# Block-summary attention and two MLPs in one kernel: mask added by a product, v summed on GpSimd, loads and steps placed anew

## Chip, cores and metric

One core of one Trainium2 chip runs the program. The time is device microseconds of one execution; the median of three runs is given, and the profile is of one further execution.

## The reference, cut to what matters

Two batches of 8 heads, 768 positions, head size 64. Keys are summarised per block of 32 by their maximum, values by their mean; each query sees keys less than 16 positions away and all 24 summaries. Then a gated MLP (512 to 1536 to 512) and a squared-relu MLP (512 to 2048 to 512) on the 1536 tokens.

```python
k_sum = k.reshape(B, H, nb, block, D).max(axis=3)
v_sum = v.reshape(B, H, nb, block, D).mean(axis=3)
scores_l = scale * np.matmul(q, k.transpose(0, 1, 3, 2))
mask_l = np.abs(pos[:, None] - pos[None, :]) < window
scores_s = scale * np.einsum('bhsd,bhnd->bhsn', q, k_sum) + np.log(block)
scores_all = np.concatenate([np.where(mask_l, scores_l, -1e9), scores_s], axis=-1)
a = np.exp(scores_all - np.max(scores_all, axis=-1, keepdims=True))
a = a / (np.sum(a, axis=-1, keepdims=True) + 1e-09)
x = np.matmul(a, np.concatenate([v, v_sum], axis=2))
g = x @ w_gate
x = (g * (1.0 / (1.0 + np.exp(-g))) * (x @ w_val)) @ w_out
h = np.maximum(x @ w_in, 0.0)
return h * h @ w2_out
```

## The kernel before

**Work and order.** The tokens are three sets of 512. Attention of a set is four pairs of heads, each with two units of 256 queries. The weights arrive as 64-bit floats in chunks; VectorE and ScalarE turn the words into fp32 by integer pieces (`convert`, L152 to L181: abs, clamp, shift, sign, low), and split each value into a high and a low fp32r part (`split_chunk`, L197), so that every product is three matmuls. Converted chunks are written to DRAM (`keep_chunk`) and read again (`load_kept`) for the later sets.

**Prologue (L516 to L623).** Attention of set 0 runs as a loop over t, written out by hand: in iteration t unit t+1 has its scores, unit t its mask and exps, unit t-1 its reciprocals, normalisation and transposes, unit t-2 the copy of the transposed weights (`turned`), unit t-3 its product with v, unit t-4 the split of the result into x high and x low. Between them stand the v sums, the k maxima (`sum_k`, `fill_k`) and the conversion of chunks 0 and 1 (`tick`). `begin` multiplies the first chunk's parts as soon as their x is there.

**Steps (L642 to L707).** Step k works on weight chunk k: 12 for each set in the gated MLP ("12"), then 16 for each set in the second MLP ("34"). A step has three slots, n = 3k, 3k+1, 3k+2: the gate product with silu (L681), the value product with g = g * p (L683) and the split of g into `hh` and `hl` (L684, L685), and the second-layer block of the step before (`second`, L486 or L488). In each slot `first`, `after` and `late` hold the attention steps of the next set, placed by `place` (L427 to L448): for pair hp of the next set s = d0 + 6 hp + 4, scores at s and s+1, product at s+9 and s+10. `pieces_of` runs the conversion of chunk k+2 and the split of chunk k+1 in the slots. All loads go out on SP's queue, in the order of the program; each engine runs its own instructions in that order too.

**v sums.** `sum_v` (L256) sums v over 32 positions with 24 matmuls of a 0/1 matrix `sel` (scaled by 1/32); `keep_v` copies the result to `vs`, and `load_vs` (L313) spreads it from there into the last 24 rows of the v tile by a DMA that repeats each row.

**Masks.** `masked` (L349) is one VectorE pass a block, which adds the mask to the scores from PSUM, writes them negated to SBUF and keeps their minimum; `exps` (L363) reads that copy.

The lines in the profile: L262 v sums, L344 scores, L357 mask pass, L368 exps, L381 and L387 normalisation, L393 transposes, L397 their copy, L405 product with v, L412 and L416 x high and low, L460 first-layer products, L209 the low part of a weight chunk, L177 and L172 the sign and low pieces, L328 and L336 k maxima, L376 reciprocal.

Of the kernel before, what the change touches and what calls it, by code (L numbers as in the profile page):

```python
# [24 lines left out]
def block_summary_attention__gated_mlp__relu2_mlp(  # L25
# [13 lines left out]
    P = 128  # L39
# [43 lines left out]

    VG = 3
    VT = 4 * S // P
    sel = const.tile([P, VG, 4 * NS], F32, name="sel")

# [168 lines left out]
    def sum_v(b, g, pool):  # L256

        n = 4 * NS
        t = vn_t.pop((b, g))
        ps = bank(pool)  # L260
        for i in range(VT):
            nc.tensor.matmul(  # L262
                ps[0:n, 0:D], sel[:, i * VG // VT, :], t[:, i * D:(i + 1) * D],
                start=(i == 0), stop=(i == VT - 1),
            )
        vs_t[b, g] = ps

    def keep_v(b, g):
        n = 4 * NS
        ps = vs_t[b, g]  # L270
        vs = vs_t[b, g] = sm_p.tile([P, D], F32, tag="vs", name="vs")
        nc.vector.tensor_copy(vs[0:n, :], ps[0:n, 0:D])

    class Pair:
# [28 lines left out]
        def load_q(self):  # L303
            self.q = att_p.tile([P, 2 * UB, P], F32, tag="q", name="q", bufs=3)
            for b, bk, at, n in self.runs():
                nc.sync.dma_start(out=self.q[:, at:at + n, :], in_=qB[b, self.hp, :, bk:bk + n, :])
# [6 lines left out]
        def load_vs(self):  # L313
            for b, bk, at, n in self.runs():
                for j in range(2):
                    h = 2 * self.hp + j
                    r = (h % 4) * NS
                    nc.sync.dma_start(
                        out=self.v[WIN:W, at:at + n, j * D:(j + 1) * D],
                        in_=vs_t[b, h // 4][r:r + NS, :].unsqueeze(1).to_broadcast([NS, n, D]),  # L320
                    )
# [26 lines left out]

        def masked(self, j):  # L349
            ps = self.st.pop(("ps", j))  # L350
            s = self.st["s", j] = att_p.tile([P, 512], F32, tag="s", name="s", bufs=3)
            m = self.st["m", j] = sm_p.tile([P, UB], F32, tag="m", name="m")
            for i in range(UB):
                bk = self.units[j][1] * UB + i
                mv = 0 if bk == 0 else (2 if bk == NBK - 1 else 1)
                c = slice(i * W, (i + 1) * W)
                nc.vector.tensor_tensor_reduce(  # L357
                    out=s[:, c], in0=ps[:, c], in1=mask[:, mv, :],
                    scale=-SCALE, scalar=3.0e38, op0=ALU.add, op1=ALU.min,
                    accum_out=m[:, i:i + 1],  # L360
                )

        def exps(self, j):  # L363
            s, m = self.st["s", j], self.st.pop(("m", j))
            r = self.st["r", j] = sm_p.tile([P, UB], F32, tag="r", name="r")
            for i in range(UB):
                c = slice(i * W, (i + 1) * W)
                nc.scalar.activation(  # L368
                    s[:, c], s[:, c], ACTF.Exp, bias=m[:, i:i + 1], scale=-1.0,
                    accum_out=r[:, i:i + 1],  # L370
                )

        def recip(self, j):
            r = self.st["r", j]
            nc.vector.tensor_scalar_add(r, r, 1e-9)
            nc.vector.reciprocal(r, r)  # L376
# [33 lines left out]
        def high(self, j):  # L410
            ts = slice(j * UT, (j + 1) * UT)
            nc.scalar.copy(self.x[0][self.hp][:, ts], self.st["po", j][:, 0:UT])  # L412
# [13 lines left out]
    def place(i, x):  # L426

        d0 = (i - 1) * 3 * F1
        pairs = [Pair(i, hp, x) for hp in range(NP)]
        for hp, p in enumerate(pairs):  # L430
            s = d0 + 6 * hp + 4
            at(first, s - 9, p.load_k)
            at(first, s - 8, p.load_q)
            at(first, s - 4, p.sum_k)
            at(first, s - 3, lambda p=p: p.fill_k(nc.vector))
            at(first, s - 4, p.load_v)
            at(first, s + 5, p.load_vs)
            for j in range(2):
                at(after, s + j, lambda p=p, j=j: p.scores(j))
                at(first, s + j + 1, lambda p=p, j=j: p.masked(j))  # L440
                at(late, s + 3, lambda p=p, j=j: p.exps(j))
                at(first, s + 6, lambda p=p, j=j: p.recip(j))
                at(after, s + 6, lambda p=p, j=j: p.norm_act(j))
                at(after, s + 7 + j, lambda p=p, j=j: p.turn(j, ps_a))
                at(first, s + 8 + j, lambda p=p, j=j: p.turned(j))
                at(after, s + 9 + j, lambda p=p, j=j: p.product(j, ps_a))
                at(first, s + 10 + j, lambda p=p, j=j: p.high(j))
                at(first, s + 10 + j, lambda p=p, j=j: p.low(j))  # L448
# [56 lines left out]
    with tc.manual_schedule():  # L505
# [15 lines left out]
        pairs[1].load_q()  # L521
        make_identity(nc, ident)
# [23 lines left out]
        load_words(0)  # L546
        pairs[2].load_k()
        pairs[2].load_q()
# [16 lines left out]

        for t in range(n_u + 4):
            if t == 0:
                go("scores", 0)
            go("high", t - 4)
            if t == 0:  # L570
                load_vn(0, 1)
                pairs[1].load_v()
            elif t == 1:
                pairs[3].load_k()
                pairs[3].load_q()
            elif t == 2:
                pairs[0].load_vs()
                pairs[1].load_vs()
                pairs[2].load_v()
                load_words(1)  # L580
            elif t == 4:
                pairs[2].load_vs()
                pairs[3].load_v()
                load_words(2)
            elif t == 5:
                pairs[3].load_vs()
            go("scores", t + 1)
            if t in (0, 2):
                sum_v(0, t // 2, ps_m)
            go("masked", t)  # L590
# [30 lines left out]
            tick(2)  # L621
# [20 lines left out]
        for k in range(NK):  # L642
# [25 lines left out]
            if kind == "12":  # L668
                h = new_h()
                for j in range(2):  # L670
# [100 lines left out]
```

## Time and profile before

| | |
|---|---|
| runs | 681.62, 683.2, 685.67 us (median 683.2) |
| the profiled execution | 683.89 us, span 681.8 us (2.1 us lie around it) |
| mean granted TensorE clock | 0.967 |
| TensorE busy | 646.6 us (95%) |
| VectorE, ScalarE, GpSimd busy | 414.3 (61%), 347.3 (51%), 13.1 us (2%) |
| DMA moved | 126.03 MB |

Times are microseconds from the span's start. PE is TensorE's matmuls and PEld its weight loads, DVE is VectorE, ACT ScalarE, POOL GpSimd, SP the queue that issues DMAs. The granted clock is the share of full speed (2.4 GHz) that TensorE was given. An fp32 matmul of this kernel shows as two records. A wait for several things is put down to the one that came last by the profile; where the engine that it names had long been done, it was another, often a DMA.

### The profile page before, as it was taken

To read this page: it belongs to the slowest core of one execution; us is meant where nothing else is said; L and a number is where in the kernel's file an instruction comes from. 1 tells how busy PE (TensorE), PEld (TensorE's weight loads), DVE (VectorE), ACT (ScalarE), POOL (GpSimd) and SP (SyncE) were. 2 spreads that over 40 slices of the span, in tenths; PEclk is the share of its full clock that TensorE was granted. 3 is DMA by queue.
4 is the path that set the end of the run, shared out by engine and by line. 5 is a ranking of instruction groups with operands and counts; after the bars stand their busy time and mean duration, and the time that the engine had idled before them with its cause. 6 is when DMAs were issued, how large, how long until landed. Compare 5 with 4: busy or idle time off the path is not lost.

```text
span 681.8 us, 9023 instructions
## 1 busy us (share of the span) xinstructions
PE 646.6 (95%) x3312; PEld 534.8 (78%) x3312; DVE 414.3 (61%) x686; ACT 347.3 (51%) x622; POOL 13.1 (2%) x26
## 2 busy tenths in 40 slices
PE   5758997979999999999999999999999999999997
PEld 5746886868788778788888888888888888888885
DVE  3277977967857666576866766444454454544443
ACT  3364476666744887674544334444444444444442
POOL 2120000000000000000000000000000000000000
PEclk9677998979999999999999999999999999999999
DMA  8998659593498587537576533222324222252211
GB/s 332 310 313 295 225 201 331 190 315 137 163 357 269 188 284 262 191 139 249 214 267 239 174 124 123 93 94 103 109 96 156 92 93 93 92 175 104 93 46 63
DMA packets 52908, 126.03 MB, mean 185 GB/s; under 512 B 9856, under 2 KB 16000, under 8 KB 51328
## 3 DMA queue, kind: packets, MB, share of 16 engines
q1 hardware_dynamic: 52864, 125.46, 53.3%
q8 instruction: 26, 0.43, 0.3%
q14 instruction: 18, 0.15, 0.1%
HBM read 103.28 MB, written 20.97 MB: 182 GB/s over the span
## 4 chain that ended last, share of the span: by engine, by line
PE 84%; DMA 6%; DVE 4%; ACT 4%; issue 2%; SPq 1%; POOLq 0%; DVEq 0%; ACTq 0%
PE bank L460 25%; PE bank L469 19%; PE bank L488 19%; PE bank L486 14%; PE bank L262 2%; DMA vn<-in_vN_dram 2%; PE bank L405 2%; PE bank L344 2%; DMA v<-vs 1%; PE bank L393 1%; DMA wf<-kept 1%; DMA q<-in_qB_dram 1%; DVE wlo L209 1%; ACT wf L158 1%; ACT s L368 1%
## 5 line engine op out<-in xcount | busy, mean ns | idle before, releaser
L209 DVE TENSOR_TENSOR wlo<-wf,whi 128x1024 fp32r<-128x1024 f32 (+2 forms) x85 | 122.0, 1435 | 50.9 <-ACT whi L208 50.2
L208 ACT CAST whi<-wf 128x1024 fp32r<-128x1024 f32 (+2 forms) x85 | 104.2, 1226 | 78.7 <-PE bank L488 50.8
L460 PE MATMUL bank<-xh,whi 128*128 128x512 f32 x288 | 116.8, 406 | 2.3 <-ACT g L681 2.3
L460 PE MATMUL bank<-xl,whi 128*128 128x512 f32 x288 | 113.6, 394 | 0.0
L460 PE MATMUL bank<-xh,wlo 128*128 128x512 f32 x288 | 113.4, 394 | 0.0
L695 DVE TENSOR_TENSOR r<-r 128x512 f32<-128x512 f32 x48 | 33.2, 692 | 87.0 <-ACT hh L694 87.0
L488 PE MATMUL bank<-whi,hl 128*128 128x512 f32 x192 | 74.8, 390 | 0.0
L488 PE MATMUL bank<-whi,hh 128*128 128x512 f32 x192 | 74.7, 389 | 0.0
L488 PE MATMUL bank<-wlo,hh 128*128 128x512 f32 x192 | 74.7, 389 | 0.0
L469 PE MATMUL bank<-xh,whi 128*128 128x512 f32 x192 | 74.7, 389 | 0.0
L469 PE MATMUL bank<-xl,whi 128*128 128x512 f32 x192 | 74.7, 389 | 0.0
L469 PE MATMUL bank<-xh,wlo 128*128 128x512 f32 x192 | 74.7, 389 | 0.0
L693 ACT ACTIVATE r<-bank 128x512 f32<-128x512 f32 x48 | 28.7, 598 | 87.3 <-PE bank L469 87.3
L460 PEld LDWEIGHTS bank<-xh,whi 128*128 128x128 f32 x288 | 55.0, 191 | 14.0 <-ACT g L681 2.7
L684 ACT CAST hh<-g 128x512 fp32r<-128x512 f32 x36 | 22.3, 619 | 85.2 <-DVE g L683 85.2
L460 PEld LDWEIGHTS bank<-xh,wlo 128*128 128x128 f32 x288 | 54.8, 190 | 11.9 <-DVE wlo L209 0.2
L460 PEld LDWEIGHTS bank<-xl,whi 128*128 128x128 f32 x288 | 55.0, 191 | 10.6
L486 PE MATMUL bank<-hh,whi 128*128 128x512 f32 x144 | 59.7, 415 | 0.0
L486 PE MATMUL bank<-hl,whi 128*128 128x512 f32 x144 | 58.0, 403 | 0.0
L486 PE MATMUL bank<-hh,wlo 128*128 128x512 f32 x144 | 57.7, 401 | 0.0
L368 ACT ACTIVATE s<-s,m 128x120 f32<-128x120 f32 x96 | 36.6, 382 | 17.2 <-DVE m L357 17.1
L177 DVE SCALAR_TENSOR_TENSOR wf<-raw,wf 128x1024 uint32<-128x1024 uint32 (+2 forms) x29 | 42.3, 1457 | 0.1
(60 smaller groups left out, 898.8 us busy)
## 6 DMA issues: line engine op xcount, KB each, us to landing
wf<-kept SPq DMA_DIRECT2D x120, 256.0 KB
raw<-in_w_dram SPq DMA_DIRECT2D x44, 512.0 KB
kept<-wf SPq DMA_DIRECT2D x28, 512.0 KB
raw<-in_w_dram SPq DMA_DIRECT2D x12, 1024.0 KB
wf<-kept SPq DMA_DIRECT2D x24, 512.0 KB
kw<-in_kW_dram SPq DMA_DIRECT2D x8, 768.0 KB
q<-in_qB_dram SPq DMA_DIRECT2D x8, 512.0 KB
vn<-in_vN_dram SPq DMA_DIRECT2D x4, 768.0 KB
```

Of the source, the lines that this page charges most:

```text
L177: nc.vector.scalar_tensor_tensor(out=w, in0=lw, scalar=29, in1=w, op0=ALU.logical_shift_right, op1=ALU.bitwise_or)
L208: lambda: nc.scalar.copy(hi[:, cs], t),
L209: lambda: nc.vector.tensor_sub(lo[:, cs], t, f32(hi[:, cs])),
L262: nc.tensor.matmul(ps[0:n, 0:D], sel[:, i * VG // VT, :], t[:, i * D:(i + 1) * D], start=(i == 0), stop=(i == VT - 1),)
L368: nc.scalar.activation(s[:, c], s[:, c], ACTF.Exp, bias=m[:, i:i + 1], scale=-1.0, accum_out=r[:, i:i + 1],)
L460: nc.tensor.matmul(p, w[a][:, c], x[i][kk], start=(kk == 0 and n == 0), stop=(kk == KD - 1 and n == 2),)
L469: nc.tensor.matmul(p, w[a][:, c], x[i][kk], start=(kk == 0 and n == 0), stop=(kk == KD - 1 and n == 2),)
L486: nc.tensor.matmul(ps[t], w[a][:, c], h[e], start=(f == 0 and n == 0), stop=(f == last and n == 2))
L488: nc.tensor.matmul(ps[t], h[e][:, t * P:(t + 1) * P], w[a][:, off:off + DM], start=(f == 0 and n == 0), stop=(f == last and n == 2),)
L684: nc.scalar.copy(h[0], g)
L693: nc.scalar.activation(r, p, ACTF.Relu)
L695: nc.vector.tensor_mul(r, r, r)
```

## The change

- **Prologue scores.** `masked_scores` adds the mask on TensorE, as a second product into the same bank (identity times mask); `tops` takes the maxima by one VectorE reduction and scales them; `masked_exps` reads the scores from PSUM. The steps keep `masked` and `exps`.
- **v sums.** `sum_v` is now three halving additions on GpSimd; `mean_v` sums the last partials by three matmuls. `vs` is one constant tile.
- **Prologue order.** SP's loads are in another order (chunk 0, k and q of pair 2, v of pair 1 and the second v group ahead of the setup; chunk 1 at t=0); `load_vs` goes to ScalarE's queue at t=0 and t=5; the second v sum moves to t=4 and t=5; chunk 0's conversion starts at t=2 and its pieces are spread by one or two an iteration.
- **Steps.** k loads at s-4 (were s-9), q at s-6 (s-8), v at s-3 (s-4), vs at s+7 (s+5); `sum_k` and `fill_k` late in s-2 (s-4, s-3), `fill_k` on GpSimd; one `recips` for two units; turn, copy and product one slot later; x high on VectorE. Weight loads move from the head of the step to slot 1, the keep from there to slot 2. In the "12" steps the sign piece moves between the cast of `hh` and the subtraction for `hl`. In step 0 the abs of chunk 2 comes behind the silu, clamp and shift in slot 1. The second batch's v loads go out in slot 0 and are summed late in slots 1 and 3.

```diff
...
-    def sum_v(b, g, pool):
-        n = 4 * NS
-        t = vn_t.pop((b, g))
-        ps = bank(pool)
-        for i in range(VT):
+    def sum_v(b, g, engine):
+        t = vn_t[b, g].rearrange("p (s c d) -> p s c d", s=VG, d=D)
+        n = VT // VG // 2
+        while n:
+            engine.tensor_add(t[:, :, 0:n, :], t[:, :, 0:n, :], t[:, :, n:2 * n, :])
+            n //= 2
+    def mean_v(b, g, pool):
+        t = vn_t.pop((b, g)).rearrange("p (s c d) -> p s c d", s=VG, d=D)
+        ps = vs_t[b, g] = bank(pool)
+        for i in range(VG):
             nc.tensor.matmul(
-                ps[0:n, 0:D], sel[:, i * VG // VT, :], t[:, i * D:(i + 1) * D],
-                start=(i == 0), stop=(i == VT - 1),
-            )
-        vs_t[b, g] = ps
+                ps[0:4 * NS, 0:D], sel[:, i, :], t[:, i, 0, :], start=(i == 0), stop=(i == VG - 1)
...
-        def load_vs(self):
+        def load_vs(self, queue):
             for b, bk, at, n in self.runs():
                 for j in range(2):
                     h = 2 * self.hp + j
                     r = (h % 4) * NS
-                    nc.sync.dma_start(
+                    queue.dma_start(
...
+        def masked_scores(self, j):
+            ps = self.st["ps", j] = bank(ps_a)
+            for i in range(UB):
+                c = slice(i * W, (i + 1) * W)
+                nc.tensor.matmul(ps[:, c], self.q[:, j * UB + i, :], self.kw[j][:, i, 0:W], start=True, stop=False)
+                nc.tensor.matmul(ps[:, c], ident, mask[:, self.variant(j, i), :], start=False, stop=True)
...
+        def tops(self, j):
+            m = self.st["m", j] = sm_p.tile([P, UB], F32, tag="m", name="m")
+            ps = self.st["ps", j]
+            nc.vector.tensor_reduce(
+                out=m, in_=ps[:, 0:UB * W].rearrange("p (n c) -> p n c", c=W), op=ALU.max, axis=AX.X
+            )
+            nc.vector.tensor_scalar_mul(m, m, -SCALE)
...
+        def masked_exps(self, j):
+            ps, m = self.st.pop(("ps", j)), self.st.pop(("m", j))
+            s = self.st["s", j] = att_p.tile([P, 512], F32, tag="s", name="s", bufs=4)
+            r = self.st["r", j] = sm_p.tile([P, UB], F32, tag="r", name="r")
+            for i in range(UB):
+                c = slice(i * W, (i + 1) * W)
+                nc.scalar.activation(
+                    s[:, c], ps[:, c], ACTF.Exp, bias=m[:, i:i + 1], scale=SCALE,
+                    accum_out=r[:, i:i + 1],
+                )
...
+        def recips(self):
+            r = self.st.pop("rr")
...
-        def high(self, j):
+        def high(self, j, copy):
             ts = slice(j * UT, (j + 1) * UT)
-            nc.scalar.copy(self.x[0][self.hp][:, ts], self.st["po", j][:, 0:UT])
+            copy(self.x[0][self.hp][:, ts], self.st["po", j][:, 0:UT])
...
             s = d0 + 6 * hp + 4
-            at(first, s - 9, p.load_k)
-            at(first, s - 8, p.load_q)
-            at(first, s - 4, p.sum_k)
-            at(first, s - 3, lambda p=p: p.fill_k(nc.vector))
-            at(first, s - 4, p.load_v)
-            at(first, s + 5, p.load_vs)
+            at(first, s - 4, p.load_k)
+            at(first, s - 6, p.load_q)
+            at(late, s - 2, p.sum_k)
+            at(late, s - 2, lambda p=p: p.fill_k(nc.gpsimd))
+            at(first, s - 3, p.load_v)
+            at(first, s + 7, lambda p=p: p.load_vs(nc.sync))
             for j in range(2):
                 at(after, s + j, lambda p=p, j=j: p.scores(j))
                 at(first, s + j + 1, lambda p=p, j=j: p.masked(j))
                 at(late, s + 3, lambda p=p, j=j: p.exps(j))
-                at(first, s + 6, lambda p=p, j=j: p.recip(j))
+                if j == 0:
+                    at(first, s + 6, p.recips)
                 at(after, s + 6, lambda p=p, j=j: p.norm_act(j))
-                at(after, s + 7 + j, lambda p=p, j=j: p.turn(j, ps_a))
-                at(first, s + 8 + j, lambda p=p, j=j: p.turned(j))
-                at(after, s + 9 + j, lambda p=p, j=j: p.product(j, ps_a))
-                at(first, s + 10 + j, lambda p=p, j=j: p.high(j))
-                at(first, s + 10 + j, lambda p=p, j=j: p.low(j))
+                at(after, s + 8 + j, lambda p=p, j=j: p.turn(j, ps_a))
+                at(late if j else first, s + 9, lambda p=p, j=j: p.turned(j))
+                at(after, s + 10 + j, lambda p=p, j=j: p.product(j, ps_a))
+                at(first, s + 11 + j, lambda p=p, j=j: p.high(j, nc.vector.tensor_copy))
+                at(first, s + 11 + j, lambda p=p, j=j: p.low(j))
...
+        load_words(0)
+        pairs[2].load_k()
+        pairs[2].load_q()
+        pairs[1].load_v()
+        load_vn(0, 1)
...
-        load_words(0)
-        pairs[2].load_k()
-        pairs[2].load_q()
...
+        sum_v(0, 0, nc.gpsimd)
         for t in range(n_u + 4):
             if t == 0:
-                go("scores", 0)
-            go("high", t - 4)
+                go("masked_scores", 0)
+            go("high", t - 4, nc.scalar.copy)
             if t == 0:
-                load_vn(0, 1)
-                pairs[1].load_v()
-            elif t == 1:
                 pairs[3].load_k()
                 pairs[3].load_q()
-            elif t == 2:
-                pairs[0].load_vs()
-                pairs[1].load_vs()
                 pairs[2].load_v()
                 load_words(1)
             elif t == 4:
-                pairs[2].load_vs()
                 pairs[3].load_v()
                 load_words(2)
-            elif t == 5:
-                pairs[3].load_vs()
-            go("scores", t + 1)
-            if t in (0, 2):
-                sum_v(0, t // 2, ps_m)
-            go("masked", t)
+            go("masked_scores", t + 1)
+            go("tops", t)
+            if t in (0, 5):
+                mean_v(0, t // 5, ps_m)
+                keep_v(0, t // 5)
+            go("recip", t - 1)
+            go("norm", t - 1)
             if t % 2 == 0 and t // 2 + 1 < NP:
                 pairs[t // 2 + 1].sum_k()
                 pairs[t // 2 + 1].fill_k(nc.gpsimd)
-            if t in (1, 3):
-                keep_v(0, t // 2)
-            go("recip", t - 1)
-            go("norm", t - 1)
+            if t == 4:
+                sum_v(0, 1, nc.gpsimd)
             go("product", t - 3, ps_c)
-            go("exps", t)
+            go("masked_exps", t)
             go("low", t - 4)
             go("turned", t - 2)
-            if t == 3:
+            if t in (0, 5):
+                pairs[t // 5 * 2].load_vs(nc.scalar)
+                pairs[t // 5 * 2 + 1].load_vs(nc.scalar)
+            if t == 2:
                 pieces += convert_chunk(0)
+                tick()
+            elif t == 3:
+                tick(2)
             elif t == 5:
                 tick(len(pieces))
                 pieces += split_chunk(0)
...
                 tick(len(pieces))
                 pieces += convert_chunk(1)
                 begin(0, 0)
+            elif t == 7:
+                keep_chunk(0)
+                begin(1, 0)
+                tick()
             elif t == 8:
-                keep_chunk(0)
                 load_words(3)
-                begin(1, 0)
+                tick()
             elif t == 9:
                 begin(0, 1)
                 begin(1, 1)
             elif t == 11:
                 begin(0, 2)
                 begin(1, 2)
-            tick(2)
+            tick()
             go("turn", t - 1, ps_c)
...
-        load_vn(1, 0)
-        load_vn(1, 1)
         for g in range(2):
-            at(after, 7 + g, lambda g=g: sum_v(1, g, ps_a))
+            at(first, 0, lambda g=g: load_vn(1, g))
+            at(late, 1 + 2 * g, lambda g=g: sum_v(1, g, nc.gpsimd))
+            at(after, 7 + g, lambda g=g: mean_v(1, g, ps_a))
             at(first, 8 + g, lambda g=g: keep_v(1, g))
         cv = {2: convert_chunk(2)}
-        cv[2][0]()
...
-            load_words(k + 4)
-            keep_chunk(k + 1)
             sp, c2 = split_chunk(k + 1), cv.pop(k + 2)
-            work = [sp[0:1] + c2[1:3], sp[1:2] + c2[3:4], c2[4:5]]
+            if k:
+                work = [sp[0:1] + c2[1:3], sp[1:2], c2[4:5]]
+            else:
+                work = [sp[0:1], sp[1:2] + c2[1:3], c2[4:5]]
             def pieces_of(*slots):
                 nonlocal ticks
                 for s in slots:
                     for f in work[s]:
                         f()
+                    if s == 1:
+                        load_words(k + 4)
                     if s == 2:
+                        keep_chunk(k + 1)
                         load_kept(k + 3)
                         cv[k + 3] = convert_chunk(k + 3)
                         cv[k + 3][0]()
...
                         nc.scalar.activation(g, p, ACTF.Silu)
+                        if k == 0:
+                            c2[0]()
                     else:
                         nc.vector.tensor_mul(g, g, p)
                         nc.scalar.copy(h[0], g)
+                        c2[3]()
                         nc.vector.tensor_sub(h[1], g, f32(h[0]))
...
```

## Rows read from the trace of the kernel before

**Rows 1.** Busy times by stretch: PE, PEld, DVE, ACT, POOL (instructions), clock, DMA share, GB/s.

```profile
6.80:59.60 52.80, 41.00 (x333) 36.16 (x333) 27.44 (x101) 22.87 (x82) 9.75 (x14) 0.74 0.95 329
72.80:174.30 101.50, 94.10 (x564) 78.23 (x563) 77.87 (x148) 65.70 (x138) 0.00 (x0) 0.93 0.68 237
112.80:119.60 6.80, 6.19 (x28) 4.84 (x28) 2.24 (x3) 6.73 (x20) 0.00 (x0) 0.50 0.93 340
140.10:146.90 6.80, 6.13 (x28) 4.96 (x28) 2.65 (x3) 6.10 (x19) 0.00 (x0) 0.50 0.95 355
146.90:676.00 529.10, 526.44 (x2541) 433.16 (x2540) 314.05 (x452) 267.01 (x431) 0.00 (x0) 1.00 0.46 158
```

**Rows 2.** Timeline, TensorE: first scores and last product of the prologue.

```profile
6.79 3.73 PE L344 MATMUL bank<-kw,q 128*128 128x120 f32 x16 [6.79 <-DVE kw L336]
...
58.89 0.69 PE L405 MATMUL bank<-a,v 120*64 120x64 f32 x16
```

**Rows 3.** Chain that ended last, in order of time: start, us, what.

```profile
21.62 7.94 PE bank L262 x48
...
73.06 2.74 PE bank L486 x12
...
103.20 10.07 DMA v<-vs
...
174.33 2.72 PE bank L486 x12
```

**Rows 4.** Groups by line and shape: operands, count, busy us, mean ns, idle before.

```profile
L357 DVE CUSTOM_DVE_ANT_0 s<-bank,mask 128x120 f32<-128x120 f32 x96 | 21.2, 277 | 3.4 <-PE bank L344 3.4
...
L262 PE MATMUL bank<-vn,sel 128*96 128x64 f32 x192 | 20.6, 278 | 3.8 <-DMA vn<-in_vN_dram 3.8
...
L177 DVE SCALAR_TENSOR_TENSOR wf<-raw,wf 128x1024 uint32<-128x1024 uint32 x17 | 21.5, 1266 | 0.1
...
L416 DVE TENSOR_TENSOR xl<-bank,xh 128x256 fp32r<-128x256 f32 x24 | 10.0, 416 | 31.5 <-ACT xh L412 31.5
...
L412 ACT CAST xh<-bank 128x256 fp32r<-128x256 f32 x24 | 8.5, 363 | 8.8 <-PE bank L405 8.8
...
L328 DVE TENSOR_REDUCE ks<-kw 128x24 f32<-128x768 f32 x8 | 7.6, 949 | 5.5 <-DMA kw<-in_kW_dram 5.5
...
L376 DVE RECIPROCAL r<-r 128x4 f32<-128x4 f32 x24 | 4.3, 178 | 0.8
```

**Rows 5.** Waits of TensorE: who waited for whom, us, times, longest.

```profile
PE bank L405 <- DVE hl L685: 3.7, 1, 3.7
...
PE bank L405 <- DMA v<-vs: 3.0, 1, 3.0
...
PE bank L344 <- ACT a L397: 2.7, 3, 1.3
```

**Rows 6.** Timeline, SP's queue: issues of vs.

```profile
103.20 3.35 SPq L318 DMA_DIRECT2D v<-vs  x4
...
130.45 3.70 SPq L318 DMA_DIRECT2D v<-vs  x4
```

**Rows 7.** Waits of SP's queue.

```profile
SPq L294 <- PE bank L344: 34.1, 3, 13.7
```

**Rows 8.** Timeline, VectorE: product g of steps 1, 2 and 3.

```profile
75.82 0.68 DVE L683 TENSOR_TENSOR g<-g,bank 128x512 f32<-128x512 f32 x1
...
87.38 0.68 DVE L683 TENSOR_TENSOR g<-g,bank 128x512 f32<-128x512 f32 x1
...
100.42 0.68 DVE L683 TENSOR_TENSOR g<-g,bank 128x512 f32<-128x512 f32 x1
```

**Rows 9.** Timeline, GpSimd and VectorE side by side in the prologue.

```profile
38.88 0.99 POOL L381 TENSOR_TENSOR s<-s,r 128x480 f32<-128x480 f32 x1 [2.35 <-DVE r L376]
...
38.94 2.01 DVE L177 SCALAR_TENSOR_TENSOR wf<-raw,wf 128x1024 uint32<-128x1024 uint32 x1
```

**Rows 10.** Waits of VectorE.

```profile
DVE hl L685 <- ACT hh L684: 28.4, 36, 3.1
```

More of the change, by code (lines that the diff above doesn't have):

```diff
@@ L86, in block_summary_attention__gated_mlp__relu2_mlp @@
     sel = const.tile([P, VG, 4 * NS], F32, name="sel")
+    vs = const.tile([P, 2, 2, D], F32, name="vs")
     def new_x():
@@ L254, in load_vn @@
         nc.sync.dma_start(out=t, in_=vN[b, g].rearrange("r m -> (r m)").rearrange("(p m) -> p m", p=P))
-    def sum_v(b, g, pool):
-        n = 4 * NS
-        t = vn_t.pop((b, g))
-        ps = bank(pool)
-        for i in range(VT):
+    def sum_v(b, g, engine):
[8 more added lines that the diff above has]
+        for i in range(VG):
             nc.tensor.matmul(
-                ps[0:n, 0:D], sel[:, i * VG // VT, :], t[:, i * D:(i + 1) * D],
-                start=(i == 0), stop=(i == VT - 1),
+                ps[0:4 * NS, 0:D], sel[:, i, :], t[:, i, 0, :], start=(i == 0), stop=(i == VG - 1)
             )
-        vs_t[b, g] = ps
     def keep_v(b, g):
[L269 to L272, printed above, removed]
+        nc.vector.tensor_copy(vs[0:4 * NS, b, g, :], vs_t.pop((b, g))[0:4 * NS, 0:D])
     class Pair:
@@ L303, in load_q @@
         def load_q(self):
-            self.q = att_p.tile([P, 2 * UB, P], F32, tag="q", name="q", bufs=3)
+            self.q = att_p.tile([P, 2 * UB, P], F32, tag="q", name="q", bufs=2)
             for b, bk, at, n in self.runs():
@@ L317, in load_vs @@
                     r = (h % 4) * NS
-                    nc.sync.dma_start(
+                    queue.dma_start(
                         out=self.v[WIN:W, at:at + n, j * D:(j + 1) * D],
-                        in_=vs_t[b, h // 4][r:r + NS, :].unsqueeze(1).to_broadcast([NS, n, D]),
+                        in_=vs[r:r + NS, b, h // 4, :].unsqueeze(1).to_broadcast([NS, n, D]),
                     )
@@ L347, in scores, with variant @@
                 )
+        def masked_scores(self, j):
[4 more added lines that the diff above has]
+                nc.tensor.matmul(ps[:, c], ident, mask[:, self.variant(j, i), :], start=False, stop=True)
+        def variant(self, j, i):
+            bk = self.units[j][1] * UB + i
+            return 0 if bk == 0 else (2 if bk == NBK - 1 else 1)
+        def tops(self, j):
[15 more added lines that the diff above has]
+                )
         def masked(self, j):
             ps = self.st.pop(("ps", j))
-            s = self.st["s", j] = att_p.tile([P, 512], F32, tag="s", name="s", bufs=3)
+            s = self.st["s", j] = att_p.tile([P, 512], F32, tag="s", name="s", bufs=4)
             m = self.st["m", j] = sm_p.tile([P, UB], F32, tag="m", name="m")
             for i in range(UB):
-                bk = self.units[j][1] * UB + i
-                mv = 0 if bk == 0 else (2 if bk == NBK - 1 else 1)
+                mv = self.variant(j, i)
                 c = slice(i * W, (i + 1) * W)
@@ L364, in exps @@
             s, m = self.st["s", j], self.st.pop(("m", j))
-            r = self.st["r", j] = sm_p.tile([P, UB], F32, tag="r", name="r")
+            if j == 0:
+                self.st["rr"] = sm_p.tile([P, 2 * UB], F32, tag="rr", name="rr")
+            r = self.st["r", j] = self.st["rr"][:, j * UB:(j + 1) * UB]
             for i in range(UB):
@@ L374, in recip @@
             r = self.st["r", j]
+            nc.vector.tensor_scalar_add(r, r, 1e-9)
+            nc.vector.reciprocal(r, r)
+        def recips(self):
+            r = self.st.pop("rr")
             nc.vector.tensor_scalar_add(r, r, 1e-9)
@@ L441, in place @@
                 at(late, s + 3, lambda p=p, j=j: p.exps(j))
-                at(first, s + 6, lambda p=p, j=j: p.recip(j))
+                if j == 0:
+                    at(first, s + 6, p.recips)
                 at(after, s + 6, lambda p=p, j=j: p.norm_act(j))
-                at(after, s + 7 + j, lambda p=p, j=j: p.turn(j, ps_a))
-                at(first, s + 8 + j, lambda p=p, j=j: p.turned(j))
-                at(after, s + 9 + j, lambda p=p, j=j: p.product(j, ps_a))
-                at(first, s + 10 + j, lambda p=p, j=j: p.high(j))
-                at(first, s + 10 + j, lambda p=p, j=j: p.low(j))
+                at(after, s + 8 + j, lambda p=p, j=j: p.turn(j, ps_a))
[3 more added lines that the diff above has]
+                at(first, s + 11 + j, lambda p=p, j=j: p.low(j))
     def run(d, n):
```

## The prediction

> **What bounds the kernel now.** I read the busy times by stretch first. From 147 us on TensorE is busy 526.4 of 529.1 us at full clock [rows 1]. What can be won lies before that, in two stretches: the prologue, which ends with its last attention product at 59.6 [rows 2], and the eight steps from the second-layer block of step 1 (73.06) to that of step 9 (174.33) [rows 3]. A step is one weight chunk k; the eight take 101.5 us.
>
> In the **prologue** TensorE is busy 41.0 of 52.8 us, but at a mean granted clock of 0.74, and VectorE only 27.4 [rows 1]. In the chain of waits one piece stands out: the 48 matmul records that sum v for heads 4 to 7, 7.94 us from 21.62 on [rows 3], all other work behind them. All 192 records of v sums take 20.6 us [rows 4]; the other three groups thus take 4.2 each, one in the prologue and two (8.4) in the steps.
>
> In the **eight steps** TensorE is busy 94.1 of 101.5 us [rows 1]. Its long waits are two: 3.0 us for the broadcast of vs, and 3.7 put down to VectorE's L685; three later ones for ScalarE's copy of a are 1.3 at most [rows 5]. I read the 3.7 as the broadcast too: SP issued vs at 103.20 and at 130.45 [rows 6], each about 10 us before a stop ended, and for the first the chain names 10.07 us of that transfer [rows 3]. Around the end of each stop the granted clock falls to 0.50 (the 1.2 GHz level) for 6.8 us, in which TensorE works 6.19 and 6.13 us [rows 1]; half of that, 6.2, is lost. The short waits lie in the stretch granted 1.00 throughout [rows 1, 5]. Why is vs late? SP's queue runs in order, and a k load in it stands up to 13.7 us, 34.1 in three times, for the scores that free its buffer [rows 7]; the weight loads, keeps and vs behind it then go out together.
>
> VectorE is the next limit. From the product g of step 1 (75.82) to that of step 2 it needs 11.56 us, to that of step 3 (100.42) 24.6 for two steps [rows 8].
>
> **The change, part by part.**
>
> *v sums.* A group falls from 48 records to 6, at 20.6/192 = 0.11 us each 0.65. In the steps TensorE drops 8.4 and gets 1.3 back. Its bare need there is then 94.1 - 8.4 - 6.2 + 1.3 = 80.8 us, 10.1 a step. The sums become three GpSimd additions of 768, 384 and 192 elements per partition: by its product of 480 elements in 0.99 us [rows 9], 1344 x 0.99/480 = 2.8 us a group. VectorE pays beside it: L177 took 2.01 us over that product [rows 9] against a mean of 1.27 [rows 4], so 0.74 of 0.99. I charge 0.75 x 2.8 = 2.1 us a group, between nothing (operations that GpSimd doesn't disturb) and the whole 2.8. The Trainium skill ("SBUF — State Buffer", Who interferes with whom) speaks against the move: the ports that these two engines share are, it says, locked for a whole instruction. By it VectorE would stand 2.8 us a group, some 3 us more over the four groups; the additions themselves are in no run here.
>
> *Prologue scores.* The mask becomes a second product of the same shape: 8 more records a unit. The first 16 took 3.73 us [rows 2], so 1.9 us a unit at worst; at 0.11 a record it is 0.9. Over eight units 7 to 15 us of TensorE, I take 11, against 7.9 + 4.2 - 1.3 = 10.8 of sums that go: even. On VectorE one reduction of 480 columns (768 take 0.95, so 0.6) with a small scaling replaces four masked passes of 0.28 that overlap [rows 4]: even, at most 0.5 a unit less. For exp from PSUM the nearest row is ScalarE's cast of 256 PSUM columns in 0.36 [rows 4]; an exp of 120 costs at most that much more than from SBUF, or something less; between the two I take no difference. The scores' bank is now held until the exps end; the scores two units on wait for that.
>
> *New waits.* mean_v on TensorE waits for GpSimd's sum, at t=0 (behind it the scores of unit 2) and t=5 (the product of unit 2). The vs transfers go to ScalarE's queue and wait for keep_v; behind them stand the next unit's exps. Eight issues at 0.84 (3.35 for four [rows 6]) are 6.7 us of ScalarE, busy 22.9 of 52.8 [rows 1]: there is room, though not at those two places. SP sheds them and issues the loads earlier; the bytes stay the same.
>
> *Prologue's end.* VectorE: 27.4 of work and 4.2 beside two sums are 31.6, from 10.5 on (first scores, 6.8 + 3.73): 42 if it never waits. TensorE: 41 us from 6.8 at the same clock: 48, less at a higher one. With the share of waits of before nothing is gained: 59.6. I take 50, nearer the two sums, since the 8 us piece goes and the conversion pieces are spread one or two to a unit: **-9.6** (-15 to 0).
>
> *Entry into the steps.* From 59.6 to 73.06 before, 13.5 us [rows 2, 3]. Now the abs of chunk 2 comes behind the silu, and sum_k and fill_k of the next set's first pair behind the low piece of chunk 2 (late in slot 2). VectorE does nearly a full step, 11.56 us [rows 8], ahead of that fill, and stands 2.1 for GpSimd's first sum; TensorE waits for the fill at the scores of slot 4, then has a unit of scores and the other product block. 16 us in place of 13.5: **+2.5** (0 to +5).
>
> *The steps.* k loads go out four slots ahead, behind the scores that free their buffer, so SP no longer stands; weight loads go out in slot 1, vs behind them and ahead of the keep, and SP runs up to a step ahead of the products. Both stops and their half clock go (3.0 + 3.7 + 6.2). But then VectorE's time for two steps sets the pace. It loses the wait of L685 for the cast, 28.4 over 36, 0.79 each [rows 10], since the sign piece now stands there: 1.6. It loses half of the recips (a reciprocal of 0.18 [rows 4], and its addition, set equal), and gains two PSUM copies of ScalarE's at 0.42 like L416 [rows 4]: 0.8. What it loses in fill_k it pays as GpSimd's disturbance. 24.6 - 1.6 - 0.4 + 0.8 = 23.4; I take 23.5. Three such pairs, and the last two steps, without masked passes, at TensorE's 10.1 each: 90.7 against 101.5: **-10.8** (-20.7 if TensorE sets the pace, -7.5 if the 24.6 stays).
>
> *Later.* turn and product move one slot on, so scores no longer share a slot with a turn for two banks; the three waits of 2.7 us [rows 5] go mostly: **-2** (-2.7 to 0). The fills and GpSimd's work there lie beside a VectorE that is busy 314 of 529 us [rows 1]; without that room they would cost what they do in the steps.
>
> **Sum.** -9.6 + 2.5 - 10.8 - 2 = -19.9. The profiled execution took 683.9, 0.7 over the median of 683.2; 664.0 less 0.7 gives **663 us**.
>
> **Rivals.**
> 1. *TensorE keeps its pace* (chance 0.17). For it: VectorE works only 77.9 of the 101.5 us [rows 1]. Against: the 11.56 and 24.6 us [rows 8]. The steps at 80.8: 9.9 less, 653.
> 2. *The prologue gains nothing* (0.13). GpSimd's sums and ScalarE's issues stand in in-order queues, and mean_v holds TensorE. For it: TensorE's 41 us at a low clock. Against: the 8 us piece does go. 9.6 more, 673.
> 3. *All taken back* (0.06): as 2, with all steps at 24.6 for two (98.4) and no later gain. 2.5 - 3.1 = -0.6: 683. The sums would have left TensorE without having set the pace.
> 4. *Slower* (0.06). VectorE, disturbed by GpSimd, comes late in every step, and TensorE stops once a step. What decides is the length of a stop: those of 1.3 us kept the clock at 1.00, those of 3.0 and 3.7 came with 0.50 for 6.8 us [rows 1, 5]. At some 2.3 us a step, with 3.1 for the clock, steps take 15.5, eight of them 124, 33 over my 90.7: 697. Against: the 23.4 us leave stops of 1.6 a step.
>
> **Numbers.** My forecast has 0.58. Faster by over 0.5% comes with it and rivals 1 and 2: 0.88; within 0.5% (3.4 us, about what a measurement of this kernel can tell from no change) 0.06; slower 0.06. The range takes in rivals 1 and 2 with part of the bounds of prologue and entry: 647 to 677. Left out are all best bounds together, and rivals 3 and 4.
>
> **What would show it.** Right: the last prologue product near 50; a wait for the fill at the entry; no long stop at a product for vs and no half clock from step 2 to 9; g of odd steps 23 to 24 us apart; 24 records of v sums. Wrong: half clock again in those steps (4), 24.6 (3), the last prologue product at 57 or later (2), steps of 10.1 (1).

## The result, and the profile after

The changed kernel takes **661.93 us** (median of four, 661.7 to 664.86) against 682.47 for the kernel before on the same chip: a ratio of 0.970, 95% interval 0.966 to 0.974. The forecast was 663. The profiled executions split as follows (us; the first column is the end of the last attention product of the prologue, the next two the starts of the second-layer blocks of steps 1 and 9; entry, eight steps and later are the stretches between these points and behind them):

| | last product | step 1 | step 9 | span | entry | eight steps | later |
|---|---|---|---|---|---|---|---|
| before | 59.6 | 72.8 | 174.2 | 681.8 | 13.2 | 101.3 | 507.6 |
| after | 53.1 | 65.3 | 154.5 | 660.0 | 12.2 | 89.2 | 505.5 |
| gain | 6.5 | | | 21.8 | 1.0 | 12.1 | 2.1 |

One profile does not fix the prologue closely: in runs 3 to 6 below, which leave its program as it is, the last product ends between 51.5 and 54.4.

In the kernel after, L445 is the product with v, L501 the first-layer products, L348 the scores in the steps, L340 `fill_k`, L263 GpSimd's sums, L733 and L736 g and `hl`, L174 the sign piece, L163 the clamp, L160 the abs, L211 the low part of a chunk, L390 the mask pass, L433 the transposes, L437 the copy of a, L729 silu. The experiments' lines are shifted a little; the operands name them.

Busy times by stretch after the change (columns as in [rows 1]): the prologue, the eight steps, two steps alone, and the rest.

```profile
6.80:53.10 46.30, 35.80 (x313) 31.68 (x313) 26.14 (x53) 22.86 (x83) 16.26 (x20) 0.89 0.98 332
65.30:154.50 89.20, 82.45 (x479) 66.20 (x479) 81.75 (x144) 63.78 (x134) 11.69 (x10) 1.00 0.84 275
104.00:126.00 22.00, 20.87 (x129) 16.84 (x129) 20.33 (x38) 16.97 (x37) 0.88 (x2) 1.00 0.96 310
154.50:655.00 500.50, 499.36 (x2375) 411.46 (x2374) 298.01 (x410) 245.46 (x383) 2.52 (x8) 1.00 0.46 158
```

The eight steps run at a granted clock of 1.00 (the 2.4 GHz level) throughout; before it was 0.93 with two stretches at 0.50. TensorE (82.45) and VectorE (81.75) are now about equally busy there. TensorE's waits in that stretch (to set beside [rows 5], which span the whole run) have none for vs left.

```profile
PE bank L433 <- DVE m L390: 3.4, 3, 1.2
PE bank L501 <- DVE wlo L211: 2.7, 2, 2.0
PE bank L501 <- ACT g L729: 0.7, 1, 0.7
```

VectorE's timeline shows g of steps 5, 6 and 7 (as [rows 8]), and behind the second the sign piece between g and `hl`:

```profile
114.94 0.68 DVE L733 TENSOR_TENSOR g<-g,bank 128x512 f32<-128x512 f32 x1
124.63 0.68 DVE L733 TENSOR_TENSOR g<-g,bank 128x512 f32<-128x512 f32 x1
125.23 1.75 DVE L174 SCALAR_TENSOR_TENSOR wf<-raw,wf 128x1536 uint32<-128x1536 uint32 x1
126.90 0.68 DVE L736 TENSOR_TENSOR hl<-g,hh 128x512 fp32r<-128x512 f32 x1
137.02 0.68 DVE L733 TENSOR_TENSOR g<-g,bank 128x512 f32<-128x512 f32 x1
```

Two steps take 22.1 us (137.02 - 114.94), not 23.5. In the prologue, where the forecast was 3 us too good, the product with v stops twice for vs (TensorE's timeline):

```profile
26.18 1.12 PE L445 MATMUL bank<-a,v 120*64 120x64 f32 x14 [2.17 <-DMA v<-vs]
44.75 1.27 PE L445 MATMUL bank<-a,v 120*64 120x64 f32 x16 [2.28 <-DMA v<-vs]
```

The chain of waits has the second of them as one long transfer, issued at 35.05 among the bulk loads:

```profile
35.05 9.56 DMA v<-vs
```

TensorE's clock is at half from 26.0 to 29.4 and from 43.0 to 49.9.

### The profile page after: what moved, and what is told of

It is laid out like the page before. It is cut to its first block, busy times and chain, and to the rows that moved or that the text cites. A ratio compares the mean times of both kernels' runs of the same rounds, so it can differ in the third digit from the quotient of the medians.

```text
span 660.0 us, 8823 instructions
## 1 busy us (share of the span) xinstructions
PE 627.9 (95%) x3208; PEld 517.1 (78%) x3208; DVE 417.9 (63%) x622; ACT 340.0 (52%) x606; POOL 40.1 (6%) x54
## 4 chain that ended last, share of the span: by engine, by line
PE 78%; DVE 9%; ACT 5%; DMA 5%; issue 2%; POOL 1%; SPq 0%; DVEq 0%; ACTq 0%; POOLq 0%
PE bank L501 22%; PE bank L510 20%; PE bank L529 19%; PE bank L527 11%; DMA kept<-wf 2%; DVE wlo L211 2%; PE bank L445 1%; DVE wf L179 1%; DMA v<-vs 1%; ACT s L403 1%; DVE wf L174 1%; ACT wf L160 1%; PE bank L348 1%; DVE wf L163 1%; PE bank L433 1%
## 5 line engine op out<-in xcount | busy, mean ns | idle before, releaser
L211 DVE TENSOR_TENSOR wlo<-wf,whi 128x1024 fp32r<-128x1024 f32 (+2 forms) x85 | 123.5, 1454 | 52.5 <-ACT whi L210 51.6
L501 PE MATMUL bank<-xh,whi 128*128 128x512 f32 x288 | 116.5, 405 | 3.8 <-ACT g L729 1.9
L501 PE MATMUL bank<-xh,wlo 128*128 128x512 f32 x288 | 113.2, 393 | 4.5 <-DVE wlo L211 4.5
L501 PE MATMUL bank<-xl,whi 128*128 128x512 f32 x288 | 112.7, 391 | 0.0
L501 PEld LDWEIGHTS bank<-xh,wlo 128*128 128x128 f32 x288 | 54.2, 188 | 18.0 <-DVE wlo L211 6.6
L501 PEld LDWEIGHTS bank<-xh,whi 128*128 128x128 f32 x288 | 54.2, 188 | 16.5 <-ACT g L729 2.9
L501 PEld LDWEIGHTS bank<-xl,whi 128*128 128x128 f32 x288 | 54.3, 189 | 10.1
L527 PE MATMUL bank<-hh,whi 128*128 128x512 f32 x144 | 57.5, 400 | 0.0
L527 PE MATMUL bank<-hl,whi 128*128 128x512 f32 x144 | 56.2, 390 | 0.0
L527 PE MATMUL bank<-hh,wlo 128*128 128x512 f32 x144 | 56.2, 390 | 0.0
L174 DVE SCALAR_TENSOR_TENSOR wf<-raw,wf 128x1024 uint32<-128x1024 uint32 (+2 forms) x29 | 41.9, 1446 | 0.3
L529 PEld LDWEIGHTS bank<-whi,hh 128*128 128x128 f32 x192 | 36.1, 188 | 7.6
```

The lines of the kernel that those rows point to most:

```text
L174: nc.vector.scalar_tensor_tensor(out=w, in0=hw, scalar=0xC0000000, in1=w, op0=ALU.bitwise_and, op1=ALU.bitwise_or)
L211: lambda: nc.vector.tensor_sub(lo[:, cs], t, f32(hi[:, cs])),
L501: nc.tensor.matmul(p, w[a][:, c], x[i][kk], start=(kk == 0 and n == 0), stop=(kk == KD - 1 and n == 2),)
L527: nc.tensor.matmul(ps[t], w[a][:, c], h[e], start=(f == 0 and n == 0), stop=(f == last and n == 2))
L529: nc.tensor.matmul(ps[t], h[e][:, t * P:(t + 1) * P], w[a][:, off:off + DM], start=(f == 0 and n == 0), stop=(f == last and n == 2),)
```

## Experiments

Each run has its ratio to the kernel before on its own chip, since that one's median moved between chips (681.7 to 684.0). The runs change the kernel after unless said otherwise.

**1. v sums back on TensorE** (48 records a group, GpSimd free):

```diff
-            engine.tensor_add(t[:, :, 0:n, :], t[:, :, 0:n, :], t[:, :, n:2 * n, :])
...
-        for i in range(VG):
+        for i in range(VT):
```

> The changed kernel with the v sums alone taken back to TensorE (24 matmuls a group). Theory: TensorE's work counts in the prologue and is mostly absorbed in the steps, because VectorE sets their pace with about 1.1 us of TensorE idle in two steps: 4 to 7 us more in the prologue and 2 to 5 in the steps, 668 to 674 us. Rival, TensorE sets the pace of the steps: all 7 us there and the prologue's, 675 or more. Rival, the sums never mattered: 664 or less.

664.55 us, 0.975 (0.971 to 0.979). The eight steps take 88.8, as before the edit (89.2); the last product comes at 56.6 in place of 53.1. The sums on GpSimd are worth some 2.6 us, all of it in the prologue; the two ratios' intervals overlap (0.971 to 0.979, 0.966 to 0.974), so even that is hardly clear of noise. This is near the last rival, and far from the theory's 668 to 674.

**2. The kernel before with only its v sums on GpSimd.**

> The kernel before with the v sums alone moved to GpSimd. Theory: the 8 us piece of the prologue goes in part (5 to 9 us), but the two stops for vs and their half clock stay in the steps, and what TensorE sheds there is paced by VectorE: 672 to 678 us. Rival, the sums are most of the gain: 664 to 668. Rival, GpSimd holds VectorE up by as much: 681 or more.

683.12 us, 1.001 (0.998 to 1.005): no change. The number is the last rival's, not its reason: VectorE is busy 78.6 us in the eight steps, against 77.9 before. The last product comes 2.8 us sooner (56.7), but the eight steps take 3.1 more. No stop for vs is among TensorE's waits in them; with less work of its own it stands at scores, three times, with a granted clock of 0.50 behind each stop:

```profile
PE bank L349 <- DVE m L362: 10.3, 3, 3.8
```

L362 is VectorE's mask pass: the longest stop ends at 101.25, and the passes that free the bank end at 101.2. For the two steps from its g at 73.73 to that at 98.33, the stretch's busy times and VectorE's waits (L158 and L161 are abs and clamp, L693 and L694 cast and `hl`):

```profile
73.73:98.33 24.60, 20.38 (x102) 16.27 (x100) 19.79 (x40) 16.15 (x34) 0.00 (x0) 0.96 0.97 344
```

```profile
DVE wf L161 <- ACT wf L158: 3.3, 1, 3.3
DVE hl L694 <- ACT hh L693: 1.4, 2, 0.7
```

The 24.6 of [rows 8] stays to the digit though TensorE lost both sums of that stretch. VectorE's 19.79 and its two waits, 4.7, are 24.5; in this stretch it never waits for TensorE, and ScalarE waits for VectorE alone. So the pace was VectorE's, and its waits for ScalarE are part of it. In the prologue TensorE stood for GpSimd's sums where it had summed before:

```profile
PE bank L270 <- POOL vn L261: 8.7, 2, 6.6
```

Part of the 6.6 is the load of v: GpSimd's second sum starts at 21.32, when its v is there, and TensorE's 7.94 us piece of [rows 3] started at 21.62 for the same reason.

**3. The sign piece back ahead of g.**

```diff
-                        c2[3]()
                         nc.vector.tensor_sub(h[1], g, f32(h[0]))
...
-                work = [sp[0:1] + c2[1:3], sp[1:2], c2[4:5]]
+                work = [sp[0:1] + c2[1:3], sp[1:2] + c2[3:4], c2[4:5]]
```

> The changed kernel with the sign piece back in slot 1 ahead of g, out of VectorE's wait between the cast of hh and the subtraction. Theory of the prediction (VectorE sets the pace, and the move saves it 0.8 us a step): two steps take 23.5 to 24 us in place of 22.1, the eight steps 94 to 96 in place of 89.2, 667 to 669. Rival (VectorE is busy only 20.3 of 22 us and has room; TensorE's own need sets the pace): two steps at 22.1 to 22.4, 661.5 to 663.

675.14 us, 0.989 (0.985 to 0.993): 1.9% of the time, more than expected. The eight steps take 95.5, the entry 16.9. Two steps (124.14 to 148.66) take 24.5; stretch and VectorE's waits:

```profile
124.10:148.60 24.50, 21.49 (x129) 16.78 (x128) 20.56 (x38) 17.15 (x36) 0.52 (x2) 1.00 0.68 227
```

```profile
DVE wf L163 <- ACT wf L160: 2.4, 1, 2.4
DVE hl L735 <- ACT hh L734: 1.4, 2, 0.7
```

In the kernel after only 1.5 of these 3.8 us is left for two steps (the view gives it for four):

```profile
DVE wf L163 <- ACT wf L160: 3.0, 2, 1.5
```

So one piece of 1.75 us, put into a wait, took away the wait for the cast (1.4) and 0.9 of that for the abs. The edit also puts the sign piece ahead of g in step 0, and TensorE stops there for 3.8 us; that stop and the clock at half were not in the expectation's price. In the kernel after and in runs 1, 6, 7, 8, 9 and 11, g of step 7 comes 22.05 to 22.08 us behind g of step 5, whatever TensorE did before: the pace is VectorE's in all of them.

**4. VectorE lighter:** the clamp is left out from step 1 on.

```diff
-                work = [sp[0:1] + c2[1:3], sp[1:2], c2[4:5]]
+                work = [sp[0:1] + c2[2:3], sp[1:2], c2[4:5]]
```

> The changed kernel without the clamp piece from step 1 on, so VectorE does 0.96 us less in each of the first set's steps (the output is then only right for weights within the clamp's bounds). Theory (VectorE sets the pace of two steps, 22.1): the eight steps shorten by 4 to 7.7 us to 81.5 to 85, TensorE's own 10.1 a step being the floor; 654 to 658. Rival (something else sets it, such as TensorE's own work and loads): within 1 us of 89.2, 661 to 662.5.

655.43 us, 0.960 (0.957 to 0.964). The eight steps fall to 82.7. In two of them TensorE never pauses:

```profile
110.50:130.80 20.30, 20.30 (x128) 16.63 (x127) 18.57 (x37) 16.99 (x37) 0.54 (x2) 1.00 0.99 329
```

This is the floor of 10.1 a step that the forecast had worked out; with the clamp it is VectorE that sets the pace.

**5. k and q loads early again.**

```diff
-            at(first, s - 4, p.load_k)
-            at(first, s - 6, p.load_q)
+            at(first, s - 9, p.load_k)
+            at(first, s - 8, p.load_q)
```

> The changed kernel (661.93) with the k and q loads of the next set back at s-9 and s-8. Theory (SP standing on a k buffer made vs late in the steps): SP stands again, at least one TensorE stop of 3 to 4 us at a product for vs returns between the block of step 1 and that of step 9 with a stretch of half clock behind it; those eight steps take 95 to 102 us in place of 89.2 and the time is 667 to 675. Rival (vs was late because of its own place, one step before its product, not because of the k loads): no stop, eight steps within 1 us of 89.2, 661 to 663.

673.99 us, 0.987 (0.981 to 0.993). The eight steps take 102.7. SP's wait and two TensorE stops, and clock at half behind each (109.0 to 115.8, 136.3 to 143.1), are back:

```profile
SPq L298 <- PE bank L348: 23.1, 2, 13.4
```

```profile
PE bank L445 <- ACT a L437: 8.3, 2, 4.3
```

The stops are put down to the copy of a, as the 3.7 of [rows 5] was to `hl`; vs was issued at 98.96 and 128.07, some 10 us ahead of each stop's end:

```profile
98.96 5.62 SPq L322 DMA_DIRECT2D v<-vs  x4
...
128.07 4.25 SPq L322 DMA_DIRECT2D v<-vs  x4
```

A third stretch at half clock, 85.1 to 88.5, has no long stop ahead of it, only two of 1.3 and 1.1 us, at 82.3 and 84.1, for ScalarE's g and VectorE's low piece. So short stops do not always leave the clock at 1.00, as those of 1.3 us in [rows 5] did.

**6. vs two slots earlier** (`s + 5`), loads left late.

> The changed kernel with vs of the next set issued at s+5 again in place of s+7, the k loads left late. Theory (the k loads made vs late): nothing changes, 661 to 663, eight steps 88 to 90 us. Rival (the place of vs counts, ahead of the weight loads of its step it goes out sooner or pushes them back): a TensorE stop over 2 us at a product or at a first-layer block returns, 665 or more; or the steps get shorter by over 1 us.

663.96 us, 0.972 (0.968 to 0.977); eight steps 89.2, no stop for vs in them. It is the k loads that made vs late (SP's wait in run 5 is at one of them), not its own place.

**7. The prologue's vs on SP's queue, at the same places** (`load_vs(nc.sync)`).

> The changed kernel with the prologue's vs transfers on SP's queue at the same two places. Theory: a queue of its own brings vs no sooner, since all transfers share the engines; ScalarE sheds eight issues (some 6.9 us), and its wait of 4.2 us at t=5 goes: 658 to 661 us. Rival, the own queue does bring vs sooner: products with v come later, 664 to 667.

667.35 us, 0.978 (0.974 to 0.982). SP gets to the transfers 7 us later than ScalarE did in the kernel after, behind its loads (first ScalarE's queue there, then SP's in this run), and TensorE stops once for 11.6 us:

```profile
13.96 1.40 ACTq L322 DMA_DIRECT2D v<-vs  x1
```

```profile
21.29 8.05 SPq L322 DMA_DIRECT2D v<-vs  x4
```

```profile
34.45 1.47 PE L445 MATMUL bank<-a,v 120*64 120x64 f32 x16 [11.59 <-issue]
```

The view names no transfer for this stop; that it is for vs follows from its place, at the first products, and its time. The rival held: ScalarE's queue is worth some 5 us. By the Trainium skill ("DMA: Bandwidth & Descriptors", Issuing engines are not separate DMA queues) all queues end on the same 16 DMA engines, and another issuer saves issue time only. These runs agree if the wait in an in-order queue is counted as issue time; run 8 shows that the right order within SP's own queue is enough.

**8. vs on SP, ahead of the bulk loads.** At t=0 and t=5 vs goes out first, then k, q, v and chunk 1 (chunk 2 at t=5).

```diff
-                pairs[t // 5 * 2].load_vs(nc.scalar)
-                pairs[t // 5 * 2 + 1].load_vs(nc.scalar)
+                pairs[t // 5 * 2].load_vs(nc.sync)
+                pairs[t // 5 * 2 + 1].load_vs(nc.sync)
+                if t == 0:
+                    pairs[3].load_k()
...
+                    load_words(1)
+                else:
+                    load_words(2)
```

> The changed kernel with the prologue's vs transfers on SP's queue, ahead of the k, q and v loads and the weight chunk that go out at t=0, and at t=5 ahead of chunk 2. Theory: the vs transfers are late because of what is queued in front of them; both stops (2.2 and 2.3 us) and the half clock from 43 to 50 us go, and ScalarE sheds the issues: 654 to 659 us. Rival, the transfers held back make the next stop: k of pair 3 or chunk 1 comes late, 661 or more.

658.71 us, 0.966 (0.962 to 0.971). The last product comes at 48.7, one vs stop of 3.2 is left, and the forecast's 50 is reached (runs 9 and 10, with the same prologue: 48.1 and 49.7). But the entry grows to 19.8, by TensorE's wait and GpSimd's timeline:

```profile
PE bank L348 <- POOL kw L340: 7.3, 1, 7.3
```

```profile
58.63 6.33 POOL L263 TENSOR_TENSOR vn<-vn 128x768 f32<-128x768 f32 x3 [13.48 <-DMA vn<-in_vN_dram]
64.91 2.00 POOL L340 COPY kw<-ks 128x96 f32<-128x96 f32 x2
```

The fill stood behind a sum whose v landed at 58.6, and the clock was at half from 62.7 to 72.9. The stop costs less than its length: VectorE worked on meanwhile, and the eight steps behind it take 84.3 in place of 89.2, so that entry and steps together lose 2.7 us.

**9. Run 8 with the next batch's sums behind that fill.**

```diff
-            at(late, 1 + 2 * g, lambda g=g: sum_v(1, g, nc.gpsimd))
-            at(after, 7 + g, lambda g=g: mean_v(1, g, ps_a))
-            at(first, 8 + g, lambda g=g: keep_v(1, g))
+            at(late, 3 + 6 * g, lambda g=g: sum_v(1, g, nc.gpsimd))
+            at(after, 9 + 6 * g, lambda g=g: mean_v(1, g, ps_a))
+            at(first, 10 + 6 * g, lambda g=g: keep_v(1, g))
```

> The kernel with vs ahead of the bulk loads (658.71), and the two v sums of the next batch moved from the ends of slots 1 and 3 to those of slots 3 and 9, their means and copies likewise, so that fill_k of the first pair is ahead of them on GpSimd. Theory (the 7.26 us stop at the entry was the fill queued behind a sum whose v had not landed): the stop falls under 2 us, no half clock from 63 to 73, entry and eight steps together 101 to 102 as in the changed kernel against 104.5, 654 to 657. Rival (the fill waits for its own k, which lands as late): the stop stays over 5 us, 658 to 659.

657.87 us, 0.966 (0.960 to 0.971). The stop is gone (entry 11.5), so the fill's place in GpSimd's queue was its cause. The eight steps take 91.0, and at 85.7 scores wait 1.5 us put down to GpSimd's sum; in time the run can't be told from run 8.

**10. Run 9 with the exps of the next set one slot later** (`at(late, s + 4, ...)`), so that ScalarE takes the abs first.

> As the run before it, and the exps of the next set one slot later (late in s+4), so that ScalarE takes the abs of the next chunk ahead of them. Theory (VectorE sets the pace at 22.1 us for two steps, 1.5 of it a wait of the clamp for that abs): two steps take 20.8 to 21.3, TensorE's own need being next, and the eight steps 3 to 5 us less than in the run before it; 650 to 653. Rival (what the exps gave up comes back as a later whi and silu): 21.8 to 22.3 and no gain, within 1 us of the run before it.

655.71 us (654.91 to 657.12), 0.963 (0.958 to 0.968), 2.2 less than run 9 on the same chip. Two steps fall from 22.1 to 21.4; the wait for the abs is gone, a smaller one for the cast is back, and TensorE is busy throughout the second pair:

```profile
99.10:120.43 21.33, 19.79 (x129) 16.26 (x128) 20.61 (x40) 17.06 (x36) 1.26 (x2) 1.00 1.02 338
120.43:141.80 21.37, 21.37 (x132) 17.52 (x131) 20.61 (x38) 17.10 (x36) 0.27 (x1) 1.00 0.71 243
```

```profile
DVE hl L739 <- ACT hh L737: 0.9, 2, 0.4
DVE g L736 <- ACT g L732: 0.2, 1, 0.2
```

The direction is the theory's, its size less: 1.8 us in the eight steps, where 3 to 5 were expected. It has the lowest median of the versions that do all the work; its interval touches that of the kernel after.

**11. The prologue's scores as before** (four mask passes, exps from SBUF).

> The changed kernel with the prologue's scores as before: mask in four VectorE passes a unit, exps from the copy in SBUF, one product a block. Theory of the prediction (the two forms cost the same, TensorE's 64 records more against VectorE's passes): the last prologue product within 2 us of 53.1, 660 to 664. Rival A (the product form pays: the passes hold VectorE ahead of the conversion pieces): 3 us or more later, 665 to 668. Rival B (the second products are dear while TensorE is at half clock): 3 us or more sooner, 657 to 659.

661.92 us, 0.972 (0.967 to 0.978); last product at 53.4. Even, as charged, as far as the prologue's spread of some 3 us lets one tell.

## Why the prediction was right, and where its terms were off

The total is partly luck: the span fell by 21.8 where the sum had 19.9, but the prologue came out 3.1 worse than forecast, the entry 3.5 better and the steps 1.3 better. Of the signs named ahead, no stop for vs in the steps, the clock there and the 24 records of v sums came true (L271, 24 of them); the last product near 50, the wait for the fill and the 23 to 24 us between g did not.

**Prologue, -9.6 forecast, -6.5 measured.** The step that failed is "SP sheds them and issues the loads earlier; the bytes stay the same". The bytes do, but the DMA engines are busy for 0.98 of this stretch, and loads issued ahead of vs delay it: 2.17 and 2.28 us of stops, and the clock at half around them. With vs ahead of the loads (run 8) the last product comes at 48.7, past the forecast's 50. "Nearer the two sums, since the 8 us piece goes" gave the sums the credit; they are 3.5 us of it (run 1), 2.8 in run 2, which the steps took back. Mask and exps are even (run 11). The other 3 us, from 59.6 to run 1's 56.6, lie in the new order of loads and pieces; no run takes these apart.

**Entry, +2.5 forecast, -1.0 measured.** The step "VectorE does nearly a full step, 11.56 us [rows 8], ahead of that fill" overlooked that the first unit's fill needs no new maxima: that unit still belongs to the first batch, whose maxima the prologue made. Its fill was done by 61.6, ahead of the scores at 64.48, and only the second unit's waited for VectorE (GpSimd's timeline; the view puts that wait down to q, but VectorE's maxima for it, L332 at 65.43, end at 66.37, where the fill starts):

```profile
55.15 6.28 POOL L263 TENSOR_TENSOR vn<-vn 128x768 f32<-128x768 f32 x3 [7.88 <-DMA vn<-in_vN_dram]
61.37 0.26 POOL L340 COPY kw<-ks 128x96 f32<-128x96 f32 x1
66.43 0.94 POOL L340 COPY kw<-ks 128x96 f32<-128x96 f32 x1 [4.81 <-DMA q<-in_qB_dram]
67.33 7.14 POOL L263 TENSOR_TENSOR vn<-vn 128x768 f32<-128x768 f32 x3
```

The wait for the fill is there once the prologue ends sooner (run 8), behind a sum, not behind VectorE. The gain of 1.0 is not clear of noise: in runs 4 to 6 the entry takes 11.5 to 14.3 us. All are short of the 16 of the forecast.

**Steps, -10.8 forecast, -12.1 measured.** Both mechanisms were shown. The stops for vs came from SP standing on a k buffer (run 5 brings them back, run 6 doesn't). VectorE then sets the pace (runs 3 and 4), so rival 1 fell for that reason. The mis-sized term is the sign piece: "24.6 - 1.6" counted the wait for the cast alone, at its mean over all steps. Here it was 1.4, and 0.9 of the wait for the abs went with it: 24.5 without the move, 22.1 with it. The forecast's other terms, +0.4 together, came to -0.1.

**GpSimd beside VectorE.** The charge was 2.8 us a sum and 0.75 of it on VectorE. A sum takes 3.56 in the prologue and 6.28 and 7.14 beside VectorE's conversion (above, and):

```profile
30.43 3.56 POOL L263 TENSOR_TENSOR vn<-vn 128x768 f32<-128x768 f32 x3
```

Over the last one VectorE's pieces are longer than the same ones elsewhere (1.75 for L211 and for L174, 0.68 for `hl`); over the one before, only L168, the shift, is (0.96 elsewhere; VectorE's timeline):

```profile
59.33 1.65 DVE L168 TENSOR_SCALAR wf<-wf 128x1536 uint32<-128x1536 uint32 x1
...
68.15 3.37 DVE L211 TENSOR_TENSOR wlo<-wf,whi 128x1536 fp32r<-128x1536 f32 x1
...
72.04 1.97 DVE L174 SCALAR_TENSOR_TENSOR wf<-raw,wf 128x1536 uint32<-128x1536 uint32 x1
73.93 1.08 DVE L736 TENSOR_TENSOR hl<-g,hh 128x512 fp32r<-128x512 f32 x1
```

That is 1.6 + 0.2 + 0.4 = 2.2 us for the last sum and 0.7 for the one before. Over the prologue's two only the small scaling L370 is longer, 0.48 and 0.86 us where it takes 0.17 elsewhere: 0.3 and 0.7. So the charge of 2.1 was right for one sum in four, and the four cost 3.9 us, not 8.4. By the rule of the Trainium skill ("SBUF — State Buffer", Who interferes with whom) a sum could have cost VectorE its whole length; the trace agrees that each engine stands for the other, not with that size.

**Later, -2 forecast, -2.1 measured**: TensorE's waits behind step 9 fall from 2.7 us, all at scores for ScalarE's copy of a, to 1.1, none of them at scores. That is as forecast, but no edit tried it alone, so the cause is only argued.

## What to carry to other kernels

An engine's pace is its work plus its waits for the next engine: put a piece that is due anyway into such a wait, and count every later wait that it shortens. In an in-order DMA queue, put a small transfer that ends a wait ahead of the bulk loads: here its place on SP's queue was worth 8.6 us (run 7 against 8), the move to another queue 5.4 (run 7 against the kernel after). A large piece of the chain (the v sums) may be worth little by itself: in run 2 the same load of v and GpSimd's 3.5 us stood where TensorE's 7.9 had been, and in the steps VectorE set the pace with or without them.

## Not expected of the hardware

GpSimd's additions themselves took twice as long beside VectorE (7.14 us against 3.56), so a sum delayed not only VectorE but also the fill queued behind it on GpSimd. And 1.2 us more a step on VectorE's path (run 3) cost 12.5 us of span, of which 1.3 lie in the prologue, where the program is the same: 4.7 at the entry, where a stop of 3.8 us came with half clock from 63.8 to 70.7, and 6.3 in the eight steps.
